# A float64 weight's low word becomes a rounded count on ScalarE and is added to the high word as integers

## The chip, the core and the metric

The kernel runs on one core of a Trainium2 chip. A core has a TensorE (PE, with its weight loads shown apart as PEld), a VectorE (DVE), a ScalarE (ACT), a GpSimd (POOL), and a SyncE (SP) whose queue issues most of the DMA transfers here. Each engine works through its own instruction stream in order and waits on semaphores for the others. The metric is the device time of one execution in microseconds (us). Half a per cent of this kernel's time is 3.1 us.

## The reference

```python
# q, k, v: (4, 8, 768, 64) float32; w_in: 512 x 2048, w_out: 2048 x 512, both float64
state = gamma * state + k_t v_t^T            # per batch and head, t = 0 .. 767
y_t   = scale * q_t state
x = y.transpose(0, 2, 1, 3).reshape(3072, 512)
h = x @ w_in
g = h * (1 / (1 + exp(-h)))                  # silu
out = (g @ w_out).astype(float32)
```

The weights are float64, because a product of `randn` with a float64 scalar stays float64. They reach the core as 64-bit words and must be turned into float32 there, to about 24 significant bits. A float64 has a sign, 11 bits of exponent and 52 of fraction: the high 32-bit word holds sign, exponent and the upper 20 bits of the fraction, the low word the other 32. A float32 keeps 23 bits of fraction, so three bits come from the low word.

## The kernel before

**Tiling.** The 768 time steps are cut into chunks c = 0 to 5 of 128 steps; one chunk of all four batches is 512 columns of x. The 2048 hidden columns are cut into slices f = 0 to 15 of 128. The attention turns 24 units (chunk, batch) into x, which is split into three parts for TensorE (high part, scaled rest, third part). Then h for (c, f) is a *product* (`multiply`, L680): twelve matmuls of 128x128 by 128x512, eight into a bank `ha` and four into a bank `hb`. `close_steps` (L692) follows: ACT copies `ha` to a tile `hs` (L694; trace name g, three buffers), VectorE subtracts `hb` (L699), ACT applies Silu (L704), and `put_g` (L710) lets SP store the tile in DRAM. The two banks of a product come in turn from three (`turn`): the `hb` of the next product is where this product's `ha` was, and the `ha` of the one after next is where this `hb` was.

**Second phase.** After all 96 products, from about 353 us, g is read back, split in three and multiplied by w_out (L1025).

**The weights.** They go through in 32 slices of 128x512: i = 0 to 15 are w_in, 16 to 31 are w_out. For each, `load_w` (L173) has SP load both words of 512 numbers per partition into a tile wf, of which there are two; `convert_steps` (L192) makes one float32 of each pair of words:

- L203, ACT: absolute value of the high word read as a float, times 65536, into tile ca
- L206, DVE: the sign bit of the high word, into cs
- L209, DVE: ca clipped to a range whose exponents a float32 holds
- L213, DVE: ca shifted left by 3, or-ed with cs: the weight cut to its upper 20 bits of fraction, as a float32
- L216, DVE: only its sign and exponent, into ca
- L219, DVE: low word x 2^-52 x that, into ca
- L224, DVE: the float sum of both, into cs for i < 16, into a tile cw for i >= 16

Each of the tags ca, cs, cw has one buffer. `split_steps` (L114) then splits a w_in slice into its three parts (L120 ACT, L123 DVE, L126 ACT, L128 DVE; trace names wi and wil). A w_out slice instead is stored as float32 in DRAM by SP (`store_w`, L289; trace name wod<-cw), to be read back and split in the second phase (`get_w`, `w_out`).

**Order of work.** PE's order is written by hand throughout. Up to L916 the order of SP, VectorE, ACT and GpSimd is also written by hand (slices 0 to 2 in `early_slice`, stepped one instruction at a time by calls `W(i)` between the attention's steps). After that a scheduler orders the other engines by priorities; `tc.issue_after` (through `queue`) keeps some instructions behind others. Slices 3 to 6 are converted in the attention's visits (`begin_w`), slices 7 to 31 behind the products listed in `takes`: slices 16 to 18 behind (0,13), (0,15) and (2,12), then five each in chunks 3 and 4 and three in chunk 5. Each slice's conversion also asks for the load of slice i+2, which can start when wf's buffer is free.

Two products are 2.72 us apart when PE is dense. `visit` and the joins and turns (L421, L439) prepare k, q and v for the remaining attention units between the products of chunks 3 and 4.

Of the kernel before, what the change touches and what calls it, by code (L numbers as in the profile page):

```python
# [13 lines left out]
FP32 = mybir.dt.float32  # L14
FP32R = mybir.dt.float32r
U32 = mybir.dt.uint32
U16 = mybir.dt.uint16
AF = mybir.ActivationFunctionType
ALU = mybir.AluOpType
# [14 lines left out]
def kernel(  # L34
# [28 lines left out]
    nc = tc.nc  # L63
    B, H, S, D = q.shape
    DM, DF = moe_w_in.shape
# [4 lines left out]
    NF = DF // 128  # L70
# [5 lines left out]
    scale = 1.0 / math.sqrt(D)  # L76
# [4 lines left out]
    def pool(name, bufs, **kw):  # L81
        return ctx.enter_context(tc.tile_pool(name=name, bufs=bufs, **kw))
# [9 lines left out]
    conv = pool("conv", 1)  # L92
# [8 lines left out]
    def bits(x):  # L101
        return float(np.array(x, np.uint32).view(np.float32))
# [89 lines left out]
    def convert_steps(i, out):  # L192

        t = staged.pop(i)
        if not wide:
            out.append(t)
            return
        words = t.rearrange("p (c w) -> p c w", w=2)
        lo, hi = words[:, :, 0], words[:, :, 1]
        p = a = conv.tile([128, DM], U32, tag="ca", name=f"ca_{i}")  # L200
        s = conv.tile([128, DM], U32, tag="cs", name=f"cs_{i}")
        with queue(evac[0] if evac else None):
            nc.scalar.activation(out=a.bitcast(FP32), in_=hi.bitcast(FP32), func=AF.Abs,  # L203
                                 scale=65536.0)
        yield
        nc.vector.tensor_scalar(out=s, in0=hi, scalar1=0x80000000, scalar2=None,  # L206
                                op0=ALU.bitwise_and)
        yield
        nc.vector.tensor_scalar(out=a.bitcast(FP32), in0=a.bitcast(FP32),  # L209
                                scalar1=bits(1024 << 20), scalar2=bits((1279 << 20) - 1),  # L210
                                op0=ALU.max, op1=ALU.min)
        yield
        nc.vector.scalar_tensor_tensor(out=s, in0=a, scalar=3, in1=s,  # L213
                                       op0=ALU.logical_shift_left, op1=ALU.bitwise_or)
        yield
        nc.vector.tensor_scalar(out=p, in0=s, scalar1=0xFF800000, scalar2=None,  # L216
                                op0=ALU.bitwise_and)
        yield
        nc.vector.scalar_tensor_tensor(out=p.bitcast(FP32), in0=lo, scalar=2.0 ** -52,  # L219
                                       in1=p.bitcast(FP32), op0=ALU.mult, op1=ALU.mult)  # L220
        yield
        w = (s.bitcast(FP32) if i < NF else
             conv.tile([128, DM], FP32, tag="cw", name=f"cw_{i}"))
        nc.vector.tensor_tensor(out=w, in0=s.bitcast(FP32), in1=p.bitcast(FP32), op=ALU.add)  # L224
        out.append(w)

    def convert_w(i):

        if patient[0]:
            waiting.append(i + W_AHEAD)  # L230
        elif i + W_AHEAD not in staged:
            load_w(i + W_AHEAD)
        out = []
        steps = convert_steps(i, out)
        for _ in range(6):
            next(steps, None)

        def rounded():
            list(steps)
            return out[0]  # L240

        return rounded

    def early_slice(i):

        out = []
        yield from convert_steps(i, out)
        yield
        steps = split_steps(i, out[0], "wi", scale, w_sb, None)
        next(steps)  # L250
        yield from steps
# [4 lines left out]
    def queue(ins):  # L256

        return ExitStack() if written[0] or ins is None else tc.issue_after(ins)
# [69 lines left out]
    for j in range(2):  # L328
        for a in range(HP):
            nc.scalar.activation(out=decay[:, j, a, :], in_=lag[:, :D], func=AF.Exp,  # L330
                                 scale=float(lg[2 * a + j]))
# [10 lines left out]
    for h in range(H):  # L342
        nc.scalar.activation(out=gk[:, 0, h : h + 1], in_=pos, func=AF.Exp,
                             scale=float(-lg[h]))
# [8 lines left out]
    for c in range(1, NC):  # L353
        nc.gpsimd.tensor_tensor(out=gk[:, c, :], in0=gk[:, c - 1, :],
                                in1=step[:, HP : HP + H], op=ALU.mult)
# [647 lines left out]
    for c in range(NC):  # L1003
# [32 lines left out]
        for b in range(B):  # L1036
# [12 lines left out]
            for i in range(n):  # L1049
                cols = ts(i, DM // n)  # L1050
                nc.vector.scalar_tensor_tensor(out=o[:, cols], in0=oa[:, cols], scalar=ONE_E,
                                               in1=o[:, cols], op0=ALU.mult,
                                               op1=ALU.subtract)
# [31 lines left out]
```

## Time and profile before

| what | value |
|---|---|
| runs | 621.35, 619.75, 622.16 us; median 621.35 |
| profiled execution, span | 619.2 us |
| median above the span | 2.15 us |
| PE busy | 602.0 us, 97% |
| VectorE busy | 424.0 us, 731 instructions |
| ACT busy | 315.2 us, 601 instructions |
| first 60 us: PE busy | 48.1 us, granted clock 0.91 |

Read it in stages: the start up to 60 us (constants, first loads, the attention's first units and three slices of weights), the products with the attention's rest and the conversions (60 to 353 us), and the second phase (353 us to the end). The page gives each engine's busy time and the span in 40 equal slices in tenths; the windows give the same by stage; the groups by form give the mean time of one kind of instruction; the waits name what ended an engine's idle time.

### The profile page before, as it was taken

The numbers are of one execution on the slowest core, as the hardware profiler recorded it, in microseconds if no ns is written. First come the engines' busy times: TensorE is split into PE (matmuls) and PEld (weight loads), VectorE is DVE, ScalarE is ACT, GpSimd is POOL, SyncE is SP. The second block draws the span as 40 slices with busy tenths as digits, with TensorE's granted clock in tenths as the row PEclk, the third lists the DMA queues.
The fourth block names the chain that finished last, engine by engine and source line by source line (L and its number), as shares of the span: only waits on it lengthen the run. The fifth ranks groups of instructions, "written<-read, shape, count | busy, mean of one in ns | idle before, by whom it ended". The sixth has DMA issues, their size and how long they took to land.

```text
span 619.2 us, 13515 instructions
## 1 busy us (share of the span) xinstructions
PE 602.0 (97%) x5384; PEld 494.0 (80%) x5384; DVE 424.0 (68%) x731; ACT 315.2 (51%) x601; POOL 29.4 (5%) x85
## 2 busy tenths in 40 slices
PE   5899999999999999999999999999999999999997
PEld 4787787888778888888788888888888888888886
DVE  4789899889988877786699783645635453654631
ACT  7568897667667656655588742312221221412311
POOL 3000000100031111120000000000000000000000
PEclk9799999999999999999999999999999999999999
DMA  9997874685699599989977542532524333442301
GB/s 191 224 227 183 224 223 154 197 242 179 218 235 231 182 252 246 291 228 270 304 228 261 190 150 68 166 106 90 184 68 131 141 103 102 139 133 89 116 1 68
DMA packets 144334, 108.88 MB, mean 176 GB/s; under 512 B 101136, under 2 KB 109584, under 8 KB 144272
## 3 DMA queue, kind: packets, MB, share of 16 engines
q1 hardware_dynamic: 141392, 102.79, 59.4%
q10 hardware_dynamic: 2880, 5.24, 2.3%
q8 instruction: 42, 0.69, 0.5%
q14 instruction: 20, 0.16, 0.1%
HBM read 66.06 MB, written 36.70 MB: 166 GB/s over the span
## 4 chain that ended last, share of the span: by engine, by line
PE 73%; DVE 5%; DMA 2%; issue 2%; ACT 2%; DVEq 0%; POOLq 0%; ACTq 0%
PE o L1025 21%; PE ha L684 18%; PE oa L1025 14%; PE hb L684 9%; PE ob L1025 7%; PE y L531 2%; DMA gd<-g 2%; DVE g L699 1%; DVE ca L219 1%; PE sc L492 1%; PE sc L482 1%; DMA wf<-in_moe_w_in_dram 0%; DVE ca L216 0%; DVE cs L224 0%; PE o L1033 0%
## 5 line engine op out<-in xcount | busy, mean ns | idle before, releaser
L684 PE MATMUL ha<-xt,wi 128*128 128x512 f32 x768 | 195.4, 396 | 1.4 <-DVE g L699 0.6
L684 PEld LDWEIGHTS ha<-xt,wi 128*128 128x128 f32 x768 | 142.9, 189 | 34.2 <-ACT wi L126 1.4
L1025 PE MATMUL o<-wo,gs 128*128 128x512 f32 x564 | 143.2, 389 | 0.0
L751 DVE TENSOR_TENSOR gs<-gr,gs 128x512 fp32r<-128x512 f32 x96 | 62.2, 686 | 90.3 <-ACT gs L749 90.3
L1025 PEld LDWEIGHTS o<-wo,gs 128*128 128x128 f32 x564 | 105.9, 188 | 21.9
L749 ACT ACTIVATE gs<-gr 128x512 fp32r<-128x512 f32 x96 | 53.6, 621 | 134.2 <-issue 131.9
L1025 PE MATMUL oa<-wo,gs 128*128 128x512 f32 x376 | 115.8, 389 | 0.0
L684 PE MATMUL hb<-xt,wi 128*128 128x512 f32 x384 | 103.0, 390 | 0.2
L699 DVE TENSOR_TENSOR g<-g,hb 128x512 f32<-128x512 f32 x96 | 65.7, 684 | 40.0 <-ACT g L694 30.2
L684 PEld LDWEIGHTS hb<-xt,wi 128*128 128x128 f32 x384 | 71.9, 188 | 16.3 <-ACT g L694 1.0
L704 ACT ACTIVATE g<-g 128x512 f32<-128x512 f32 x96 | 60.4, 629 | 46.1 <-DVE g L699 46.1
L1025 PEld LDWEIGHTS oa<-wo,gs 128*128 128x128 f32 x376 | 70.6, 188 | 14.8
L1025 PE MATMUL ob<-wo,gs 128*128 128x512 f32 x188 | 73.7, 392 | 0.0
L694 ACT ACTIVATE g<-ha 128x512 f32<-128x512 f32 x96 | 56.8, 592 | 29.4 <-PE ha L684 13.9
L752 DVE SCALAR_TENSOR_TENSOR gs<-gs 128x512 fp32r<-128x512 f32 x96 | 62.1, 684 | 0.0
L1025 PEld LDWEIGHTS ob<-wo,gs 128*128 128x128 f32 x188 | 35.3, 188 | 8.7 <-DVE o L1043 1.6
L203 ACT ACTIVATE ca<-wf 128x512 f32<-128x512 f32 x32 | 21.4, 668 | 9.5 <-DVE cw L224 5.0
L219 DVE SCALAR_TENSOR_TENSOR ca<-wf,ca 128x512 f32<-128x512 uint32 x32 | 22.7, 710 | 0.5
L1042 ACT ACTIVATE o<-o 128x512 f32<-128x512 f32 x10 | 6.0, 600 | 33.4 <-PE o L1025 33.0
L213 DVE SCALAR_TENSOR_TENSOR cs<-ca,cs 128x512 uint32<-128x512 uint32 x32 | 22.1, 691 | 0.9
L500 DVE TENSOR_TENSOR am<-sc,decay 128x512 f32<-128x512 f32 x24 | 16.5, 686 | 8.6 <-PE sc L492 8.6
L531 PE MATMUL y<-qt,mid 64*64 64x64 f32 x384 | 20.3, 224 | 0.9 <-POOL token L386 0.9
(105 smaller groups left out, 572.1 us busy)
## 6 DMA issues: line engine op xcount, KB each, us to landing
gd<-g SPq DMA_DIRECT2D x96, 256.0 KB, 3.6
gr<-gd SPq DMA_DIRECT2D x96, 256.0 KB, 2.7
wf<-in_moe_w_out_dram SPq DMA_DIRECT2D x16, 512.0 KB, 4.3
out_dram<-o ACTq DMA_DIRECT2D x20, 256.0 KB, 2.1
wf<-in_moe_w_in_dram SPq DMA_DIRECT2D x16, 256.0 KB, 4.1
wf<-in_moe_w_in_dram SPq DMA_DIRECT2D x32, 128.0 KB, 4.3
kf<-in_k_dram SPq DMA_DIRECT2D x16, 256.0 KB, 4.1
qf<-in_q_dram SPq DMA_DIRECT2D x16, 256.0 KB, 4.1
```

What stands on the lines that cost most here:

```text
L203: nc.scalar.activation(out=a.bitcast(FP32), in_=hi.bitcast(FP32), func=AF.Abs, scale=65536.0)
L213: nc.vector.scalar_tensor_tensor(out=s, in0=a, scalar=3, in1=s, op0=ALU.logical_shift_left, op1=ALU.bitwise_or)
L219: nc.vector.scalar_tensor_tensor(out=p.bitcast(FP32), in0=lo, scalar=2.0 ** -52, in1=p.bitcast(FP32), op0=ALU.mult, op1=ALU.mult)
L531: i = nc.tensor.matmul(yp[ts(e, D), o, a, :], lhsT=lhsT, rhs=rhs, start=(e, o) not in started, stop=True, skip_group_check=True).ins
L684: nc.tensor.matmul(hb if i == 2 else ha, lhsT=w_sb[f][:, i, ts(kk, 128)], rhs=xt[c][:, i, kk, :], start=kk == 0 and i != 1, stop=kk == KIN ...
L694: copied[:] = [nc.scalar.activation(out=hs, in_=ha, func=AF.Copy, scale=ONE_E).ins]
L699: taken_out[:] = [nc.vector.tensor_tensor(out=hs, in0=hs, in1=hb, op=ALU.subtract).ins]
L704: nc.scalar.activation(out=hs, in_=hs, func=AF.Silu)
L749: nc.scalar.activation(out=t[:, 0, :], in_=g, func=AF.Copy, scale=HALF)
L751: nc.vector.tensor_tensor(out=t[:, 1, :], in0=g, in1=high, op=ALU.subtract)
L752: nc.vector.scalar_tensor_tensor(out=t[:, 2, :], in0=t[:, 1, :].bitcast(FP32), scalar=-1.0 / EPS, in1=high, op0=ALU.mult, op1=ALU.add)
L1025: nc.tensor.matmul(o, lhsT=g, rhs=wo[f][:, i, :], start=f == 0 and i != 1, stop=f == NF - 1 and i != 0)
```

## The change

The low word gets an operation of its own on ACT (new L210): it is converted from integer to float, scaled by 2^-27, and 2^25 is added. The spacing of float32 numbers at 2^25 is 4, so the result is 2^25 plus a rounded number of such steps: its bits are those of 2^25 plus the low word's count in units of the float32's last place. The high word is scaled by 2^-3 instead of 2^16 and clipped to a range shifted by the same 152 exponents, and the sign comes in by exclusive or. The sum of the two words' bits as 32-bit integers is then the rounded float32: the bits of 2^25 carry the exponent offset of 152 back. The mask (L216) and the multiplication (L219) are gone. The count r lives in the tile cw for every slice; for w_out slices the sum is written over it, and for w_in slices into cs. Three empty steps keep the number of steps that the hand-written order counts.

In the built program the integer addition is a VectorE instruction over 128x1024 halves of type uint16.

```diff
-        p = a = conv.tile([128, DM], U32, tag="ca", name=f"ca_{i}")
+        a = conv.tile([128, DM], U32, tag="ca", name=f"ca_{i}")
         s = conv.tile([128, DM], U32, tag="cs", name=f"cs_{i}")
+        r = conv.tile([128, DM], U32, tag="cw", name=f"cw_{i}")
         with queue(evac[0] if evac else None):
             nc.scalar.activation(out=a.bitcast(FP32), in_=hi.bitcast(FP32), func=AF.Abs,
-                                 scale=65536.0)
+                                 scale=2.0 ** -3)
         yield
         nc.vector.tensor_scalar(out=s, in0=hi, scalar1=0x80000000, scalar2=None,
                                 op0=ALU.bitwise_and)
         yield
+        nc.scalar.activation(out=r.bitcast(FP32), in_=lo, func=AF.Copy, scale=2.0 ** -27,
+                             bias=2.0 ** 25)
         nc.vector.tensor_scalar(out=a.bitcast(FP32), in0=a.bitcast(FP32),
-                                scalar1=bits(1024 << 20), scalar2=bits((1279 << 20) - 1),
+                                scalar1=bits(872 << 20), scalar2=bits((1127 << 20) - 1),
                                 op0=ALU.max, op1=ALU.min)
         yield
         nc.vector.scalar_tensor_tensor(out=s, in0=a, scalar=3, in1=s,
-                                       op0=ALU.logical_shift_left, op1=ALU.bitwise_or)
-        yield
-        nc.vector.tensor_scalar(out=p, in0=s, scalar1=0xFF800000, scalar2=None,
-                                op0=ALU.bitwise_and)
-        yield
-        nc.vector.scalar_tensor_tensor(out=p.bitcast(FP32), in0=lo, scalar=2.0 ** -52,
-                                       in1=p.bitcast(FP32), op0=ALU.mult, op1=ALU.mult)
-        yield
-        w = (s.bitcast(FP32) if i < NF else
-             conv.tile([128, DM], FP32, tag="cw", name=f"cw_{i}"))
-        nc.vector.tensor_tensor(out=w, in0=s.bitcast(FP32), in1=p.bitcast(FP32), op=ALU.add)
-        out.append(w)
+                                       op0=ALU.logical_shift_left, op1=ALU.bitwise_xor)
+        yield
+        yield
+        yield
+        w = s if i < NF else r
+        nc.vector.tensor_tensor(out=w, in0=s, in1=r, op=ALU.add)
+        out.append(w.bitcast(FP32))
```

## The prediction

> **What bounds the kernel now.** I read the page's busy shares and its 40 slices first, then the windows, to see which engine sets the pace in which stage.
>
> ```profile
> PE 602.0 (97%) x5384; PEld 494.0 (80%) x5384; DVE 424.0 (68%) x731; ACT 315.2 (51%) x601; POOL 29.4 (5%) x85
> PE   5899999999999999999999999999999999999997
> DVE  4789899889988877786699783645635453654631
> ACT  7568897667667656655588742312221221412311
> PEclk9799999999999999999999999999999999999999
> ```
>
> ```profile
> 0.00:60.00 60.00, 48.12 (x1152) 39.63 (x1152) 45.08 (x83) 41.90 (x103) 5.77 (x49) 0.91 0.97 211
> 60.00:175.00 115.00, 113.87 (x1077) 92.09 (x1080) 102.72 (x186) 83.62 (x178) 2.42 (x7) 1.00 0.70 208
> 175.00:353.00 178.00, 177.62 (x2020) 146.52 (x2011) 142.30 (x246) 120.46 (x197) 21.23 (x30) 1.00 0.89 244
> ```
>
> The windows give window, length, then busy time of PE, its weight loads, VectorE, ScalarE and GpSimd, then granted clock, DMA share and GB/s. TensorE is full from 60 us on. In 60 to 175 VectorE is nearly full too (102.7 of 115), so it can still be late there. The first 60 us miss 11.9 us of PE, with the DMA engines at 0.97. All the weights are converted before 353 us, so the last 266 us hold nothing that the change touches.
>
> Next I looked for holes in PE after 60 us: PE's waits, and the timeline, comparing each matmul's start with the one before.
>
> ```profile
> 99.65 1.20 PE L684 MATMUL ha<-xt,wi 128*128 128x512 f32 x4 [0.41 <-ACT wi L126]
> 170.92 2.12 PE L684 MATMUL ha<-xt,wi 128*128 128x512 f32 x8 [0.61 <-DVE g L699]
> 203.65 1.07 PE L684 MATMUL hb<-xt,wi 128*128 128x512 f32 x4
> 206.37 1.07 PE L684 MATMUL hb<-xt,wi 128*128 128x512 f32 x4
> ```
>
> The last two lines, the hb groups of successive products, are 2.72 us apart: the dense period of a product. Against dense issue I find these holes after 60 us: 0.75 at 97.7 to 99.6 (slice 6's low part comes late along L224, L120, L123, L126), 0.35 near 139 (ACT's copy of ha waited for a g store), 0.87 at 170 (L699 late behind a nearly gapless run of conversion on VectorE, 142 to 170), 0.35 near 269 (below), and 0.47 at 303, which is a GpSimd fence that the change leaves alone. Everything that a faster VectorE can win in the dense part is 0.75 + 0.35 + 0.87 + 0.35 = 2.3 us.
>
> **The change part by part.** Its prices are in the groups by form (count | busy, mean ns | idle before):
>
> ```profile
> L203 ACT ACTIVATE ca<-wf 128x512 f32<-128x512 f32 x32 | 21.4, 668 | 9.5 <-DVE cw L224 5.0 <-DMA wf<-in_moe_w_out_dram 2.8 <-DVE cs L224 1.7
> L219 DVE SCALAR_TENSOR_TENSOR ca<-wf,ca 128x512 f32<-128x512 uint32 x32 | 22.7, 710 | 0.5
> L216 DVE TENSOR_SCALAR ca<-cs 128x512 uint32<-128x512 uint32 x32 | 13.8, 431 | 0.4
> L224 DVE TENSOR_TENSOR cw<-cs,ca 128x512 f32<-128x512 f32 x16 | 11.6, 728 | 0.2
> L224 DVE TENSOR_TENSOR cs<-cs,ca 128x512 f32<-128x512 f32 x16 | 11.0, 690 | 0.4
> L512 DVE TENSOR_TENSOR state<-mid,sc 128x256 f32<-128x256 f32 x20 | 8.3, 414 | 0.4
> ```
>
> *Removed:* L216 and L219, 0.431 + 0.710 = 1.14 us of VectorE a slice.
>
> *The new add.* In the built program the uint32 add is a custom VectorE instruction over 128x1024 uint16 halves; no row of before has that form. Lower bound: 0.69, as L224, if two halves pass per step. Upper bound: the sum rows of 256 and 512 elements, 414 and 690 ns, have a slope of 276 per 256, so 1024 elements one at a time give 690 + 552 = 1.24. Two passes of that, 2.48, would be the far end. I take 0.69 to 1.24, the nearer end being the plain row of the same bytes: VectorE saves 1.14 a slice, at worst 1.14 - 0.55 = 0.59. Over 32 slices that is 36 us (or 19) of VectorE's 424. At 2.48 a slice would instead cost 0.6 more.
>
> The Trainium skill, page "VectorE: DVE Perf Modes", section "What auto-detection actually checks", states that an operation whose tensors are all 16-bit with unit step can run at two elements a cycle. By that rule the add stands at the 0.69 end; by the row of one element at a time it would stand at 1.24. The holes' sum is the same by both as long as VectorE saves something, and no run here shows the form yet.
>
> *The new ScalarE operation* r (low word to a rounded count) reads the same strided 128x512 words as L203, so 0.67 us; 32 of them are 21.4 us on an engine that is busy 0.73 and 0.68 of the two dense windows. Its busy time fits. What matters is its wait: r writes the cw tile, of which there is one. For slices 17 to 31 it must therefore wait until the store of slice i-1 (L289) has landed, and ACT is in order: the ha copies (L694), Silu (L704), splits and joins queue behind it. Before, only L224, late in VectorE's chain, had that wait. For slices 1 to 16 r waits only for the previous VectorE add. The clip and xor keep the prices of L209 and L213. L206 stays.
>
> How long the store takes is in the view of the wod tile:
>
> ```profile
> L289 SPq DMA_DIRECT2D wod<-cw x16: 319/327/1484, 164.4 to 341.1; - x16
> DMA to landing us min/median/max: 2.3/4.0/6.5
> ```
>
> and what ACT may lose is seen in its own timeline and waits:
>
> ```profile
> 267.84 0.68 ACT L203 ACTIVATE ca<-wf 128x512 f32<-128x512 f32 x1 [2.12 <-DVE cw L224]
> ACT g L694 <- DMA gd<-g: 10.9, 8, 2.9
> ```
>
> The first line is the hole near 269: ACT stood 2.12 us and PE lost 0.35. The rule behind it: the three banks rotate, so the ha copy must be done before hb of the next product starts, 2.72 us after its own. In the rows around 205 the copy ends 0.53 before that (205.24 + 0.60 against 206.37). A stall of ACT of s just ahead of a copy costs PE about s - 0.5; between copies, nothing up to about 1.5.
>
> *Where r falls in the built order.* PE's and GpSimd's orders are unchanged; on ACT r stands soon after the slice's L203. Slices 0 to 16: no store to wait for, 0. Slice 17: stall 1 to 2 us near 166, just fitting, 0. Slice 18: r stands behind the copy of product (1,13) and would wait some 2.6 us for the store of 17, whose own add falls near 170; the copy of (1,14) is then late: 0.65. Slice 19: store 18 lands near 203, in front of a copy and the 2.7 us of joins (1.36 each): 0.5 to 1.0. Slice 20: about 3 us near 212, where the copy just fits, 0, or 2 with the 6.5 us landing. Slices 21 to 31 have takes 8 to 11 us apart and most stores land first: 0 to 1 together. Losses: 0.65 + 0.75 + 0.3 + 0.3 = 2.0 us, bounds 0 (every store early) and 5 (landings at 6.5).
>
> *Gains.* The four holes, 2.3, less the one at 269, which the r wait may keep: 1.9 to 2.3. I take 2.2.
>
> *SP's queue.* The load of slice i+2 is now released by r and L206 instead of L219, some 2 us earlier, so it moves ahead of g stores and some k and v loads. SP issues from 0.32 us upward each; the transfers are the same 373. A g store delayed by a load that still waits on r delays the next copy (eight copies waited for a g store, up to 2.9 us). Bounds: -0.35 (the hole at 139, counted above) to +1. I take 0.2.
>
> *The first 60 us.* VectorE saves 3 x 1.1 for slices 0 to 2, but k, q and v loads are saturated there and PE waits for a GpSimd step of 4.2 us; 0 to 0.5 gain, I take 0.2. The clock row has its one low digit at slices of 15 to 31 us (granted 0.50 from 22.3 to 32.6). Eight matmuls took 3.59 us at 29.48 and 1.98 at 92.25; if VectorE's new timing ends that stretch or opens another, 0.45 of the 9.1 us that PE is busy in it, 4.1 us at most, go either way. I take 0, since the waits ahead of it are on GpSimd and DMA.
>
> The page "TensorE: Matmul & The Clock Gate", section "Part 1: The HAM clock gate", states that an idle window of some 3.4 us drops the clock to half. It speaks against a change that opens such a gap at the start; by it the sum would be up to 4.1 higher if the new ScalarE waits made one, by the rows as they stand 0.
>
> **Sum.** -2.2 + 2.0 + 0.2 - 0.2 = -0.2 us on a span of 619.2. The median of the runs, 621.35 (619.75 to 622.16), is 2.15 above that span, so about 621.1 us. Half a per cent is 3.1 us, about what a measurement of this kernel can tell from no change: faster means below 618.2, slower above 624.5.
>
> **The rivals.**
> *A. Forecast: holes closed, ACT's store waits open others* (0.47): 619.3 to 623.
> *B. Only gains* (0.20): the stores land before r is reached. -2.3 to -2.5 and up to 1 from the start: 617.9 to 619. For it: 32 slices save VectorE time, and each add, so each store, comes 1.1 us earlier. Against it: r stands three VectorE operations earlier than L224 did, which spends that and more.
> *C. ACT becomes the late engine* (0.23), the slower side: r blocks behind the store in most of slices 17 to 31, landing 4.0 after an issue that itself may wait. It decides once r blocks more than 2 us just ahead of a copy; eight of fifteen slices at 0.5 to 0.9 give 4 to 7 us, and the holes at 170 and 269 stay, so only 0.9 is won: 624.5 to 627.5. For it: a landing up to 6.5. Against it: the wide spacing of slices after 212 us. An add of 2.48 us would join this case, in 120 to 175, where VectorE has no room.
> *D. The low clock at 22 to 33 us moves* (0.10, either way): down to 617.0 or up to 625.2.
> That the add is not cheaper at all belongs to C; that nothing moves since PE is full ends inside A.
>
> **Chances.** Faster by over 0.5%: a half of B, 0.10, half of D, 0.05, and 0.02 of A: 0.17. Slower: C, 0.23, half of D, 0.05, and 0.02 of A: 0.30. The rest, 0.53, is within. Range: just below B's lower end, 617.5, to past C's middle, 626.3; A alone is 619.3 to 623.
>
> **What would show it.** VectorE busy down 19 to 36 us, ACT up 21, PE busy unchanged. The wait of 0.61 at 170 and of 0.41 at 99.65 gone. A new wait row of r on ACT ended by the DMA wod<-cw, and PE waits at hb or ha ended by ACT L694 near 171, 203 and 213. In the groups the add at 0.69 or 1.24. Wrong if r shows no such wait (then B), if it shows ten or more of 2 us or longer (C), if the clock row changes in its second digit (D), or if the add's mean is above 1.3 us.

## The result, and the profile after

The changed kernel takes 622.75 us (median of 20 runs, 620.36 to 628.71) against 619.18 us for the kernel before (median of 20, 617.15 to 623.72): a ratio of 1.0067, 95% interval 1.0044 to 1.0089. It is slower by some 4 us, where 0.2 us less was forecast. Two more comparisons gave 1.0096 (1.0065 to 1.0128) and 1.0106 (1.0080 to 1.0131). So the direction was wrong, although the time lies inside the range. That it even lies inside the forecast's own 619.3 to 623 is luck: the prediction started from three runs of before with a median of 621.35, and the 20 runs of this comparison have 619.18.

An execution can spend some microseconds of the first 60 at half the TensorE clock or not: from 20 to 40 us the granted clock was 0.74 in the profile of before, 1.00 in that of the changed kernel and 0.91 in that of the changed kernel run once more. The mean granted clock is 0.995 over the 20 runs of the changed kernel and 0.994 to 0.997 in the sets of runs of before that list it. So two single spans, here 619.2 and 619.8, say little, and places are compared below from 61 us on.

The page of the changed kernel, busy time and slices:

```profile
PE 601.1 (97%) x5384; PEld 494.0 (80%) x5384; DVE 392.5 (63%) x667; ACT 331.9 (54%) x633; POOL 28.6 (5%) x85
PE   6799999999999999999999999999999999999997
DVE  3888888678676666656599583645635453654631
ACT  7688898778665667766598641312221221412311
PEclk9999999999999999999999999999999999999999
```

VectorE did lose its work: 31.5 us of busy time and 64 instructions. ScalarE has 16.7 us more. The groups of the changed kernel, by form (count | busy, mean ns | idle before):

```profile
L210 ACT ACTIVATE cw<-wf 128x512 f32<-128x512 uint32 x32 | 21.3, 664 | 19.0 <-DMA wod<-cw 19.0
L222 DVE CUSTOM_DVE_ANT_0 cw<-cs,cw 128x1024 uint16<-128x1024 uint16 x16 | 11.0, 690 | 2.2 <-ACT cw L210 1.9
L222 DVE CUSTOM_DVE_ANT_0 cs<-cs,cw 128x1024 uint16<-128x1024 uint16 x16 | 11.0, 689 | 0.5
```

Both operations cost what the lower bounds said: the count 0.66 us, the integer sum 0.69. What is new is the last figure of the first line: 19.0 us in which ScalarE stood at r until a store of cw had landed. The waits of ScalarE from 60 to 353 us, then those of TensorE in the same window:

```profile
ACT g L702 <- DVE g L697: 33.9, 44, 1.7
ACT cw L210 <- DMA wod<-cw: 19.0, 9, 3.9
ACT g L692 <- PE ha L682: 11.8, 23, 1.4
ACT g L692 <- DMA gd<-g: 2.3, 3, 1.1
```

```profile
PE hb L682 <- ACT g L692: 3.9, 4, 1.9
PE y L529 <- POOL token L384: 0.3, 1, 0.3
```

The waits of before on VectorE (0.6) and on the low part (0.4) are gone, as is most of ScalarE's wait for g stores (10.9 to 2.3). In their place TensorE now waits four times for ScalarE's copy of ha. Both kernels issue the same 5384 matmuls in the same order, so the start of the n-th can be compared. A *hole* is time that TensorE loses against dense issue. The table gives start after minus start before, and what it changes by in each stretch (times are those of before):

| stretch, us | difference at its end | change | what happened there |
|---|---|---|---|
| to 61 | -2.38 | | start; the profile of before had the low clock |
| 61 to 161 | -3.24 | -0.86 | holes at 98 and 139 gone, small losses near 90 |
| 161 to 198 | -3.57 | -0.33 | hole at 170 (0.87) gone, a new one at 168 (0.69) |
| 198 to 211 | -0.70 | +2.87 | holes of 2.21 and 0.74 |
| 211 to 263 | -0.70 | 0 | |
| 263 to 289 | +0.47 | +1.17 | hole of 1.60 where before had 0.35 |
| 289 to the end | +0.56 | +0.09 | |

From 61 us on the changed kernel loses 2.94 us; in its two other profiles 2.73 and 4.84. The largest loss, row by row on ScalarE of the changed kernel (start, duration, then in brackets the idle time before it and its releaser):

```profile
196.43 0.58 ACT L585 ACTIVATE xt<-y 128x512 fp32r<-128x512 f32 x1
200.91 0.66 ACT L210 ACTIVATE cw<-wf 128x512 f32<-128x512 uint32 x1 [3.89 <-DMA wod<-cw]
201.47 0.58 ACT L692 ACTIVATE g<-ha 128x512 f32<-128x512 f32 x1
```

on VectorE and in SP's queue, where the store that it waits for comes from:

```profile
194.15 0.69 DVE L222 CUSTOM_DVE_ANT_0 cw<-cs,cw 128x1024 uint16<-128x1024 uint16 x1
```

```profile
192.54 0.73 SPq L189 DMA_DIRECT2D wf<-in_moe_w_out_dram  x1
193.37 2.31 SPq L430 DMA_TRANSPOSE kw<-kp  x1
195.77 0.53 SPq L708 DMA_DIRECT2D gd<-g  x1
196.39 0.38 SPq L287 DMA_DIRECT2D wod<-cw  x1
```

and on TensorE:

```profile
198.72 1.52 PE L682 MATMUL ha<-xt,wi 128*128 128x512 f32 x6
202.10 1.19 PE L682 MATMUL hb<-xt,wi 128*128 128x512 f32 x4 [1.86 <-ACT g L692]
```

Read backwards: hb started at 202.10 because the copy of ha came at 201.47; the copy came then because r stood in front of it until 200.91; r stood because the sum of the slice before, ready at 194.84, was issued as a store only at 196.39, behind a transposing load and a g store, and landed 4.5 us later. ScalarE did nothing in these 3.9 us, from 197.0 to 200.9, and VectorE was busy for 0.7 of them; it was one instruction in an in-order stream that waited for a transfer.

### The profile page after: what moved, and what is told of

It is laid out like the page before. It is cut to its first block, busy times and chain, and to the rows that moved or that the text cites. A ratio compares the mean times of both kernels' runs of the same rounds, so it can differ in the third digit from the quotient of the medians.

```text
span 619.8 us, 13492 instructions
## 1 busy us (share of the span) xinstructions
PE 601.1 (97%) x5384; PEld 494.0 (80%) x5384; DVE 392.5 (63%) x667; ACT 331.9 (54%) x633; POOL 28.6 (5%) x85
## 4 chain that ended last, share of the span: by engine, by line
PE 90%; ACT 3%; DVE 3%; DMA 2%; issue 1%; SPq 0%; POOL 0%; DVEq 0%; POOLq 0%; ACTq 0%
PE ha L682 25%; PE o L1023 21%; PE oa L1023 14%; PE hb L682 13%; PE ob L1023 7%; PE y L529 4%; DMA wod<-cw 2%; PE sc L480 2%; PE sc L490 2%; PE kp L454 1%; ACT g L692 1%; PE qp L454 1%; DVE am L498 1%; PE o L1031 0%; ACT kt L437 0%
## 5 line engine op out<-in xcount | busy, mean ns | idle before, releaser
L682 PE MATMUL ha<-xt,wi 128*128 128x512 f32 x768 | 193.2, 393 | 0.9 <-ACT xt L585 0.7
L692 ACT ACTIVATE g<-ha 128x512 f32<-128x512 f32 x96 | 56.9, 593 | 17.8 <-PE ha L682 11.8
L210 ACT ACTIVATE cw<-wf 128x512 f32<-128x512 uint32 x32 | 21.3, 664 | 19.0 <-DMA wod<-cw 19.0
L204 ACT ACTIVATE ca<-wf 128x512 f32<-128x512 f32 x32 | 21.5, 671 | 4.4 <-DVE cs L216 2.9
L498 DVE TENSOR_TENSOR am<-sc,decay 128x512 f32<-128x512 f32 x24 | 16.5, 689 | 10.6 <-PE sc L490 10.5
L216 DVE SCALAR_TENSOR_TENSOR cs<-ca,cs 128x512 uint32<-128x512 uint32 x32 | 22.1, 691 | 0.9
```

The source lines that it names most:

```text
L498: mask = nc.vector.tensor_tensor(out=am[n], in0=sc, in1=decay, op=ALU.mult).ins
L682: nc.tensor.matmul(hb if i == 2 else ha, lhsT=w_sb[f][:, i, ts(kk, 128)], rhs=xt[c][:, i, kk, :], start=kk == 0 and i != 1, stop=kk == KIN ...
L692: copied[:] = [nc.scalar.activation(out=hs, in_=ha, func=AF.Copy, scale=ONE_E).ins]
```

## The experiments

Theory 1: the loss is r's wait for the store, because it stands on ScalarE ahead of the copies. Theory 2: the count's time on ScalarE is the loss. All ratios are to runs of the kernel before on the same chip, with 95% intervals; the last column is the change of the matmuls' start from 61 us to the end against the profile of before, from one profiled execution each. Those of the changed kernel are among the quicker of their sets (621.53 against a median of 622.75, 622.39 against 626.17, 624.03 against 627.53), so they can show less than the ratios do.

| run | ratio | waits for transfers at the conversion, us (times) | from 61 us on |
|---|---|---|---|
| the changed kernel | 1.0067 (1.0044 to 1.0089) | r on wod<-cw 19.0 (9) | +2.9 |
| changed_again | 1.0096 (1.0065 to 1.0128) | r on wod<-cw 18.6 (10) | +2.7 |
| pair_changed | 1.0106 (1.0080 to 1.0131) | r on wod<-cw 23.0 (10) | +4.8 |
| new_w_in_only | 0.9993 (0.9965 to 1.0021) | no r on wod | +0.6 |
| new_w_out_only | 1.0047 (1.0017 to 1.0076) | r on wod<-cw 18.2 (10) | +6.4 |
| wait_alone | 1.0082 (1.0055 to 1.0110) | r on wod<-cw 21.5 (13) | +7.0 |
| operation_alone | 1.0059 (1.0036 to 1.0082) | none new | +4.4 |
| operation_without_ties | 1.0041 (1.0012 to 1.0071) | none new | +4.4 |
| r_behind_xor | 1.0070 (1.0030 to 1.0111) | r on wod<-cw 22.1 (10) | +7.7 |
| sum_into_cs | 0.9944 (0.9911 to 0.9976) | VectorE on wod<-cs 1.9 (1) | -1.9 |
| sum_into_cs_again | 0.9978 (0.9954 to 1.0003) | VectorE on wod<-cs 1.7 (1) | -1.1 |
| pair_sum_into_cs | 0.9976 (0.9954 to 0.9997) | VectorE on wod<-cs 1.6 (1) | +0.6 |
| r_in_place_behind_abs | 0.9919 (0.9885 to 0.9953) | VectorE on wod<-cw 1.4 | -1.0 |
| r_in_place_behind_abs_again | 0.9990 (0.9961 to 1.0019) | VectorE on wod<-cw 0.5 | +1.2 |
| two_cs_tiles | 1.0012 (0.9981 to 1.0044) | none on wod; a copy on a g store 3.2 | +4.6 |
| without_count | 1.0030 (0.9995 to 1.0064) | L203 on wod<-ca 14.4 (9) | +2.4 |
| r_on_gpsimd_w_out | 1.0112 (1.0071 to 1.0154) | r on wf loads 69.0, on GpSimd | +9.2 |
| two_sum_tiles | 1.0278 (1.0232 to 1.0324) | L203 on wod<-ca 16.5, on wf 17.7 | +20.3 |
| r_in_place | 1.0330 (1.0298 to 1.0362) | r on wf loads 46.0 (23) | +20.7 |

**The changed kernel once more**, beside the first kernels that were made from it.

> The changed kernel itself, on the chip and beside the runs of the kernel before that the other three of this set share. By the first comparison 1.0044 to 1.0089; theory 1 (r's store wait on ScalarE) expects again TensorE holes of 4 to 5 us in all near 169, 200, 205 and 268 us.

1.0096, with the holes where they were: 2.29 us near 200, 0.77 near 205, 1.21 near 269.

**One part of the change alone.** The slices of w_in have no store, those of w_out have one.

```diff
+    def convert_steps(i, out):
+        return (new_steps if i < NF else old_steps)(i, out)     # new_w_in_only
+        return (new_steps if i >= NF else old_steps)(i, out)    # new_w_out_only
```

> Slices 0 to 15 by the changed conversion, slices 16 to 31 by the one before. No slice's r then waits for a store. Theory 1: ratio 0.996 to 0.999, no hole at 200, 205; the hole of 0.35 near 269 stays as before. Theory 2: ratio 1.002 to 1.005, with the loss before 60 us.

> Slices 0 to 15 by the conversion before, slices 16 to 31 by the changed one. Theory 1: holes as in the changed kernel between 165 and 270 us, 3.5 to 4.5 us in all, and ratio 1.005 to 1.009. Theory 2: ratio 0.998 to 1.002.

The w_in half alone makes no measurable difference, the w_out half alone loses 0.47%. The w_out run shows the same place as in the changed kernel, and something that its hole brought along. Its TensorE clock over the windows 195 to 225, 200 to 215 and 203 to 215 us (window, length, busy times, granted clock, DMA share, GB/s):

```profile
195.00:225.00 30.00, 28.04 (x353) 22.76 (x352) 19.77 (x36) 18.54 (x31) 2.20 (x4) 0.94 0.80 196
200.00:215.00 15.00, 13.04 (x132) 10.25 (x134) 7.62 (x14) 8.24 (x13) 0.23 (x2) 0.89 0.58 151
203.00:215.00 12.00, 10.04 (x119) 7.77 (x121) 6.63 (x11) 7.97 (x12) 0.23 (x2) 0.86 0.41 137
```

Before had 1.00 from 200 to 214. Behind a hole of 2.3 us at 203 the matmuls came 0.43 us apart for a while, where they come 0.23 apart when dense. More on this below.

**The wait without the saving.** The kernel before, with the count added for the w_out slices into cw and overwritten later:

```diff
+        r = None if i < NF else conv.tile([128, DM], FP32, tag="cw", name=f"cw_{i}")
...
+        if r is not None:
+            nc.scalar.activation(out=r, in_=lo, func=AF.Copy, scale=2.0 ** -27,
+                                 bias=2.0 ** 25)
...
-             conv.tile([128, DM], FP32, tag="cw", name=f"cw_{i}"))
+        w = s.bitcast(FP32) if i < NF else r
```

> The kernel before, with all its VectorE operations, plus for slices 16 to 31 a ScalarE operation of the new kind that writes the low word's count into cw and is then overwritten by L224. It has the new wait and the new ScalarE time and none of VectorE's saving. Theory 1: since each store is issued about 1 us later than in the changed kernel, the holes are as large or larger, 4 to 7 us, ratio 1.006 to 1.012, with a wait of ScalarE on wod<-cw of 19 us or more. Theory 2: sixteen operations of 0.66 us on an engine that is two thirds busy, 0.998 to 1.003.

1.0082, with 21.5 us of the new wait in 13 places: as theory 1 said. But sixteen ScalarE operations came with it, so the operation was measured without the wait, first into cs:

```diff
+            if i >= NF:
+                nc.scalar.activation(out=s.bitcast(FP32), in_=lo, func=AF.Copy,
+                                     scale=2.0 ** -27, bias=2.0 ** 25)
```

> The kernel before plus, for slices 16 to 31, the ScalarE operation alone: the count is written right behind the absolute value into cs, which VectorE's sign mask then overwrites. It has the ScalarE time of wait_alone (1.0082) without its wait for the store. Theory 1: ratio 0.998 to 1.003. Theory 2: 1.005 or more.

Theory 1 expected next to nothing and 0.59% was lost. In this kernel VectorE's sign mask waits for the new operation, so it was done again with nothing tied to it:

```diff
+        if i >= NF:
+            with queue(made):                      # made: the absolute value, L203
+                spare = conv.tile([128, DM], mybir.dt.uint8, tag="cd", name=f"cd_{i}")
+                nc.scalar.activation(out=spare, in_=lo, func=AF.Copy, scale=2.0 ** -29)
```

> The kernel before plus, for slices 16 to 31, a ScalarE operation on the low words right behind the absolute value, into a spare tile of bytes that nothing reads: the ScalarE time of operation_alone without any engine waiting for its result and without a wait for a store. Theory 1: ratio 0.998 to 1.003, dense part within 1.5 us of before. Theory 2 (ScalarE's time costs as such): 1.004 or more.

Still 0.41% (0.12 to 0.71). So in a kernel without VectorE's saving ScalarE's time is not free: here theory 2 is right, theory 1 missed. The time was not lost mainly at the copies, though. TensorE's waits from 60 to 353 us, the first three lines:

```profile
PE hb L688 <- DVE xt L597: 1.5, 1, 1.5
PE ha L688 <- DVE g L703: 1.3, 2, 0.7
PE hb L688 <- ACT g L698: 0.9, 1, 0.9
```

Against before, the matmuls fell back by 1.6 us where VectorE was late with a split of x, by 0.9 where it was late with a subtraction of `hb`, and by 0.9 where ScalarE's copy was late. The two intervals of wait_alone and of this run do not separate what the wait adds on top. That has to come from the kernels that keep the count and lose the wait.

**The count kept, the wait taken away.** The smallest edit stores the sum of the w_out slices from cs instead of cw. The operations are the same; r now waits only for VectorE's sum of the slice before, and the wait for the store falls on VectorE's sign mask. With the wait r's place changed too: the scheduler moved it up on ScalarE, near 200 us from behind Silu and a split to right behind the absolute value (195.39 us in sum_into_cs, 200.91 in the changed kernel). So these kernels show what the wait costs together with the place that it forces on r.

```diff
-        w = s if i < NF else r
+        w = s
```

> The changed kernel with the sum of the w_out slices written into cs and stored from there. r then waits only for the add of the slice before; the wait for the store moves to VectorE's sign mask of the next slice (L207), at nearly the same time. Theory 1: VectorE's L697 is due only before ha of the product after next, so VectorE has one product (2.72 us) more of slack than ScalarE's copy: holes under 1.5 us in all, ratio 0.997 to 1.001. Theory 2: ratio 1.003 to 1.007.

> The kernel that stores from cs, once more, beside two_cs_tiles: 0.9911 to 0.9976 in the first comparison. Theory 1: again below 1.000, with no wait of r on wod<-cs. If the first result was chance, 1.003 or more, as the changed kernel.

0.9944 and 0.9978: faster than the kernel before in the first, and just not beyond the interval in the second (0.9954 to 1.0003); both lie below what theory 2 said. The line of r in the first of the two, from the groups by form, and all that is left of TensorE's waits from 60 to 353 us:

```profile
L210 ACT ACTIVATE cw<-wf 128x512 f32<-128x512 uint32 x32 | 21.3, 666 | 0.1
```

```profile
PE y L529 <- POOL token L384: 0.3, 1, 0.3
```

r costs what it did and no longer waits, and no line of hb waits for L692. The pair on one chip:

> The changed kernel beside the one that stores from cs, on one chip. Theory 1 (the store wait on ScalarE): 1.005 to 1.010, and TensorE loses 2.5 to 3.5 us after 61 us against the profile of before, at the same places as in its first two profiles.

> The changed kernel with the sum stored from cs. Theory 1: below pair_changed by 0.7 to 1.2%, at 0.994 to 0.999 of before, and TensorE gains 1 to 2 us after 61 us. Theory 2 (the count's ScalarE time, which both have): within 0.3% of pair_changed.

627.53 and 619.99 us: 7.5 us, 1.2% of 621.47, for the tile that is stored. Here are the first lines of ScalarE's waits from 30 to 353 us in the two, pair_changed first:

```profile
ACT g L702 <- DVE g L697: 33.0, 46, 1.7
ACT cw L210 <- DMA wod<-cw: 23.0, 10, 5.1
ACT g L692 <- PE ha L682: 9.4, 17, 1.4
```

```profile
ACT g L702 <- DVE g L697: 37.4, 42, 2.4
ACT g L692 <- PE ha L682: 20.3, 30, 1.5
ACT kt L437 <- DMA kw<-kp: 3.6, 1, 3.6
```

In the second a copy of ha waits more often for TensorE, which is as it should be; its one hole, 2.6 us near 205, has another cause, a transposing load that came 3.6 us late for ScalarE's join. Its change of +0.6 stands on that hole, so the expected gain of 1 to 2 us was not seen in this profile; pair_changed lost 4.8 where 2.5 to 3.5 was expected.

The other way is to write the count over the low words in wf, so that no tile of a store is touched by ScalarE:

```diff
-        r = conv.tile([128, DM], U32, tag="cw", name=f"cw_{i}")
-        nc.scalar.activation(out=r.bitcast(FP32), in_=lo, func=AF.Copy, scale=2.0 ** -27,
-                             bias=2.0 ** 25)
+        nc.scalar.activation(out=lo.bitcast(FP32), in_=lo, func=AF.Copy, scale=2.0 ** -27,
+                             bias=2.0 ** 25)
...
-        w = s if i < NF else r
+        r = lo
+        w = s if i < NF else conv.tile([128, DM], U32, tag="cw", name=f"cw_{i}")
```

> The count r is written over the low words in the wf tile itself, so ScalarE no longer waits for the store of the slice before; only VectorE's add waits for cw, as in the kernel before. Theory 1 (r's store wait on ScalarE is the loss: the changed kernel lost 2.15, 0.72 and 1.17 us of TensorE near 200, 205 and 268 us): these three holes are gone, the wait of L210 on the DMA wod<-cw (19.0 us, 9 times) is gone, and the ratio to before is 0.996 to 0.999, with 1.2 to 2 us won from the holes at 98, 139 and 170. Theory 2 (the second ScalarE operation itself, or its place in the start, is the loss): still 1.003 to 1.007. In both the add reads every other word; it stays 0.69 us if its speed does not need a dense operand, and goes to about 1.24 us if it does.

3.3% slower. Freed from cw, r had nothing left that held it back, and the scheduler put it far forward on ScalarE, in front of its own slice's absolute value, where it waited for the load of wf. The line of r in this run, from the groups by form:

```profile
L209 ACT ACTIVATE wf<-wf 128x512 f32<-128x512 uint32 x32 | 21.4, 668 | 46.2 <-DMA wf<-in_moe_w_out_dram 25.5 <-DMA wf<-in_moe_w_in_dram 20.5
```

One wait for a transfer had been replaced by a longer one. Ordered behind the absolute value, r can not run ahead of the load:

```diff
+        with queue(made):
+            nc.scalar.activation(out=lo.bitcast(FP32), in_=lo, func=AF.Copy, scale=2.0 ** -27,
+                                 bias=2.0 ** 25)
```

> r in the wf tile again, but ordered behind the slice's absolute value (L203) on ScalarE, so that the load has landed before r is reached; in the run of r in place without that order ScalarE stood 46.2 us at r for the loads, in 23 waits. Theory 1 (store wait on ScalarE): no wait of r on wod<-cw or on wf, no TensorE hole of 0.7 us or more at 200, 205 and 268 us; ratio 0.994 to 0.999. Theory 2 (the second ScalarE operation itself costs the time): ratio 1.002 to 1.006, with holes where L692 is late without any DMA wait ahead of it. Theory 3 (the wf tile is released later, at the add, and loads come late): ratio over 1.002 with waits of L203 on wf<-in_moe_w.

> The best kernel so far (0.9885 to 0.9953) beside other runs of the kernel before. Theory 1: again below 1.000, 0.990 to 0.998, with no wait of r for a transfer. If it was chance: 1.000 or more.

```profile
L210 ACT ACTIVATE wf<-wf 128x512 f32<-128x512 uint32 x32 | 21.4, 669 | 0.0
L223 DVE CUSTOM_DVE_ANT_0 cw<-wf,cs 128x1024 uint16<-128x1024 uint16 x16 | 11.0, 690 | 1.7 <-DMA wod<-cw 1.4
```

This is the first of the two runs: no idle time at r, and 1.4 us of VectorE's sum waiting for the store. 0.9919 in the first comparison, and 0.9990 (0.9961 to 1.0019) in the second, which is no difference and outside the 0.990 to 0.998 expected. The second profile again has a hole near 208 us where a copy of ha was late (1.8 us), without any wait of r. Holes near 200 to 213 us thus have other causes as well: the profiles of pair_sum_into_cs (2.6) and two_cs_tiles (1.9) have one too, and those of the first two sum_into_cs have none. What shows the price of r's wait is the ratios: 1.0067, 1.0096 and 1.0106 with it, 0.9919 to 0.9990 in the five runs of the two kernels without it.

**Tries that moved the wait elsewhere.** Each of these has a wait for a transfer on an in-order engine at another place.

```diff
+        with queue(shifted):                                          # r_behind_xor
+            nc.scalar.activation(out=r.bitcast(FP32), in_=lo, func=AF.Copy, scale=2.0 ** -27,
+                                 bias=2.0 ** 25)
```

> The changed kernel with r still in cw, but ordered behind the shift and xor on VectorE, some 1.5 to 2 us later. Theory 1: the store has had that much longer to land; the wait of r on wod<-cw falls from 19.0 us to 4 to 10 us, and the holes from about 4 us to 0.5 to 2.5; ratio 0.998 to 1.004. But r now stands in the chain of the conversion (0.66 us and two semaphores between xor and add), so slice 6's low part may be late at 98 us by about 1 us. Theory 2: unchanged, 1.005 to 1.008.

The wait did not shrink to 4 to 10 us, it grew to 22.1, so the 1.0070, which theory 2 gave too, separates nothing. ScalarE's order differs from the changed kernel's in two places only, both before 43 us; r stays in front of the same copies. The sum of the slice before was ready at 197.61; SP issued its store at 201.30, behind a transposing load of 2.81 us and a g store; r started at 206.46, after 6.69 us of waiting.

```diff
+        if i >= NF:                                                   # r_on_gpsimd_w_out
+            nc.gpsimd.tensor_scalar(out=lo.bitcast(FP32), in0=lo, scalar1=2.0 ** -27,
+                                    scalar2=2.0 ** 25, op0=ALU.mult, op1=ALU.add)
```

> r in place; for slices 16 to 31 it is made by GpSimd instead of ScalarE, for slices 0 to 15 by ScalarE behind the absolute value. GpSimd is busy 5%. If one operation takes 1.1 us (its 128x1024 copy of 16-bit numbers took 1.13) the w_out part costs ScalarE nothing, and theory 1 and 2 both give 0.994 to 0.999; if GpSimd holds VectorE back or takes more than 3 us, holes at L697 and at the joins appear and the ratio is over 1.003.

The operation is cheap, 0.86 us on average (median 0.65), on an idle engine. But GpSimd is in order too: r waited there 69.0 us for loads of wf, and the tokens that release TensorE's products of y stand behind it. TensorE's waits over the whole run, the first line of the view (1.2 us in the kernel before):

```profile
PE y L534 <- POOL token L389: 6.6, 6, 2.3
```

Then three kernels with more room in the tiles:

```diff
-        a = conv.tile([128, DM], U32, tag="ca", name=f"ca_{i}")       # two_sum_tiles
+        a = conv.tile([128, DM], U32, tag=("ca", "cw")[i % 2], name=f"ca_{i}")
...
-        nc.vector.scalar_tensor_tensor(out=s, in0=a, scalar=3, in1=s,
+        nc.vector.scalar_tensor_tensor(out=a, in0=a, scalar=3, in1=s,
...
+        r, w = lo, a
+        nc.vector.tensor_tensor(out=w, in0=a, in1=r, op=ALU.add)
```

> r in place in the wf tile behind the absolute value; the xor and the sum are written into the tile of the absolute value, which alternates between ca and cw. So neither ScalarE nor VectorE waits for the store of the slice before, only for the one two slices back. Theory 1: no wait on wod in either engine, the hole of 0.6 us that r in place left near 205 is gone, ratio 0.990 to 0.996. Theory 2 (the second ScalarE operation itself costs): no better than 1.000.

> As the kernel with two sum tiles, without the count: the low word is left out (the sum adds the sign word instead, with the clip and scale of the kernel before), so the 32 operations of 0.67 us are gone from ScalarE and VectorE's work is the same. Theory 1: the count without a wait is free, so within 0.3% of two_sum_tiles. Theory 2: faster than it by 0.4% or more.

Neither has an r that waits. The first loses 2.8%, the second, without the low word, 0.3%, with 1.000 inside its interval. The absolute value, which now had two tiles, moved forward on ScalarE and waited in r's place, in two_sum_tiles:

```profile
L203 ACT ACTIVATE ca<-wf 128x512 f32<-128x512 f32 x32 | 21.3, 667 | 34.2 <-DMA wod<-ca 16.5 <-DMA wf<-in_moe_w_out_dram 10.1 <-DMA wf<-in_moe_w_in_dram 7.6
```

In without_count the same line waited 21.6 us for transfers. The 2.5% between these two can therefore not be put down to the count's own time, and the question they were made for stays unanswered by them.

```diff
-        s = conv.tile([128, DM], U32, tag="cs", name=f"cs_{i}")       # two_cs_tiles
+        s = conv.tile([128, DM], U32, tag="cs", name=f"cs_{i}", bufs=2)
...
+        r, w = lo, s
```

> r in place behind the absolute value, the sum written into cs for all slices, and the room of cw given to a second cs. The store of a slice then holds back only VectorE's sign mask two slices later, and ca still orders the absolute value behind VectorE's xor of the slice before. If the store wait is what costs the changed kernel its time (theory 1), no wait on wod is left in any engine, and the ratio is 0.989 to 0.995, as good as r in place behind the absolute value (0.9919) or better. If any loosening of a ScalarE operation moves it in front of a transfer, as L203 in the run with two sum tiles (34.2 us idle in front of it, 1.0278), a wait on wf or wod of over 10 us appears on ScalarE and the ratio is over 1.000.

No wait on wod is left, and still 1.0012: theory 1 missed here. In its profile, which is of the longest of its 12 executions (626.94 us, median 621.54), the copy at 212.38 stood 3.24 us for a g store: SP had issued a wf load, the wod store and a v load in front of it. Whether this order of transfers is what took the gain back was not tested.

## Why the prediction was wrong

- **What bounds the kernel, and the four holes: right.** The holes at 98, 139 and 170 went. From 61 to 198 us the changed kernel gained 1.2 us, sum_into_cs, without the wait, 2.0.
- **The prices of the operations: right, at the lower ends.** 0.69 us for the sum and 0.66 for the count. VectorE's busy time fell by 31.5 us (19 to 36 forecast), ScalarE's rose by 16.7 (21 forecast). The rule of the Trainium skill, page "VectorE: DVE Perf Modes", section "What auto-detection actually checks", put the sum at the 0.69 end, as was measured; with the count in place the sum read its operand from every other 32-bit word and still took 0.690 us.
- **The step that failed: the losses on ScalarE ("Where r falls in the built order"), 2.0 us.** The mechanism, the tile and most of the slices were right; the sizes were not. Slice 18: 0.65 forecast, 0.69 measured. Slice 19: 0.75 forecast, 2.87 measured over its stretch (4.76 in pair_changed). Slice 20: 0.3 forecast, 0 measured. Slices 21 to 31: 0.3 forecast, one of them, near 268, had a hole of 1.60. That is some 5 us in place of 2.0. From 61 us on the gains, losses and SP's queue were to cancel (-2.2 + 2.0 + 0.2); the profile lost 2.9. The store was priced by its landing (4.0; it took 4.5), but from the sum to the landing went 6.1 us, since SP issued it 1.6 us after the sum, behind a transposing load and a g store, and r had been reached 3.9 us before it landed. That time in the queue, behind the other transfers, stood in no term of the sum; only rival C spoke of an issue that may wait.
- **"Its busy time fits": not safe as a zero.** Sixteen such operations cost 0.41% (0.12 to 0.71) in the kernel before, although ScalarE is free for a third of the time on average. The changed kernel has 31.5 us less work on VectorE, and with all 32 counts but without the wait it came out at 0.9919 to 0.9990; whether the count's own time costs it anything was not shown.
- **Rival D came, but elsewhere.** The low clock at the start differed between the changed kernel's own profiles. But the hole that r makes can bring its own, which no step had priced (last section). The term of -0.2 for the first 60 us can not be read for the same reason.
- **The rival C** named the right point of decision, more than 2 us just ahead of a copy, but needed half of the slices for it. r waited nine times, six of them for 2 us or longer, where ten were to be C's sign; a few places were enough.

What stays open: losses of 2.7 to 4.8 us explain the profiles, while the medians of the second and third comparison differ by 6 to 7 us. The runs' granted clocks account for some of the rest. Of the 20 runs of the changed kernel, the nine with a clock of 0.997 or more have a median of 621.4 us and the other eleven 625.3. In the second comparison the runs with at least 0.997 differ by 4.0 us (622.6, three runs, against 618.6, 20 runs of before), and six of the nine changed runs lie under that clock, but only six of 26 of before. The hole near 200 was 2.21, 2.29 and 3.43 us in three profiles, and the largest brought the low clock with it. That this hole is what lowers the clock in the runs that were not profiled is likely but was not shown.

## What to carry to other kernels

When an operation moves to another engine, look first at the tile that it writes and at who still reads it: a wait for a transfer that was harmless at the end of one engine's chain became a stall for everything behind it on an in-order engine whose copies free TensorE's banks. Price such a wait from the moment the data is ready to the landing, with the issue queue in between, and not by the transfer alone. And the scheduler here moved operations forward when a dependence was gone (r in r_in_place, the absolute value in two_sum_tiles); if the next thing that one depends on is a transfer, tie it behind an operation that already had to wait for that.

## What the runs showed of the hardware

**Some holes of 2 to 5 us in a dense TensorE brought half the clock with them, others did not.** In pair_changed r stood 5.13 us and TensorE 3.1, and the matmuls after it took twice as long:

```profile
198.72 1.98 PE L682 MATMUL ha<-xt,wi 128*128 128x512 f32 x8
203.78 2.07 PE L682 MATMUL hb<-xt,wi 128*128 128x512 f32 x4 [3.09 <-ACT g L692]
205.66 2.52 PE L682 MATMUL ha<-xt,wi 128*128 128x512 f32 x8
208.01 1.07 PE L682 MATMUL hb<-xt,wi 128*128 128x512 f32 x4
```

Four matmuls of hb took 2.07 us right behind the hole and 1.07 one product later. The windows 200 to 206 and 206 to 210 us of this run show the granted clock:

```profile
200.00:206.00 6.00, 2.91 (x9) 2.05 (x8) 1.98 (x3) 3.42 (x4) 0.00 (x0) 0.78 0.66 199
206.00:210.00 4.00, 4.00 (x17) 3.27 (x16) 2.11 (x4) 2.36 (x6) 0.00 (x0) 0.90 0.33 125
```

In the changed kernel's first profile, with a hole of 2.21 us at the same place, these windows have 1.00; in r_behind_xor, with 4.6 us of waiting, 207 to 211 us ran at 0.50. The Trainium skill, page "TensorE: Matmul & The Clock Gate", section "Part 1: The HAM clock gate", puts the idle window that throttles at some 3.4 us. The wait of 4.6 us agrees with that. But waits of 3.1 us here, of 2.0 in new_w_out_only (0.57 from 206 to 210 us) and of 1.9 in two_cs_tiles (0.54 from 213 to 215) were enough too, while 2.6 us in pair_sum_into_cs and 1.9 in the changed kernel left the clock at 1.00. So here the length of the hole alone does not decide.

**The 32-bit integer sum over 16-bit halves ran at the speed of a 512-element operation**, 690 ns for 1024 halves, whether its operand was dense or took every other word.
